# Two attention decoders on one core: the output projection's accumulator in two half-length column groups

## The chip, the cores and the metric

The kernel runs on one core of one Trainium2 chip. The core has a matrix engine (TensorE, rows PE and PEld in the profile, the second for its weight loads), a vector engine (DVE), a scalar engine (ACT), GpSimd (POOL), an engine that here only issues DMAs and waits (SP), and 16 DMA engines that carry every transfer whichever engine issued it. The metric is the device time of one execution in microseconds (us); the figure for a kernel is the median of several runs.

## The reference

Two independent decoding steps of attention, A and B, for four requests (one new token each). Their outputs lie side by side, A in columns 0 to 511 and B in columns 512 to 1023 of the result.

```
def attend(x, k_cache, v_cache, wq, wo, H, Hkv, window):      # A: H=32, Hkv=8, last 2048 keys;  B: H=32, Hkv=32, all 8192 keys
    q = (x @ wq)                                              # x: 4 x 1 x 512, wq: 512 x 4096 -> 32 heads of 128
    k, v = last `window` keys and values, repeated H/Hkv times
    p = softmax(q k^T / sqrt(128))
    o = p v                                                   # 4 x 32 x 1 x 128
    return o.reshape(4, 1, 4096) @ wo                         # wo: 4096 x 512
out = concatenate([attend(A...), attend(B...)], axis=-1)      # 4 x 1 x 1024, bf16
```

All tensors are bf16. B's keys and values are 2 x 256 MiB, and every byte of them is read once.

## The kernel before, in words

**Chunks.** The work is cut into 8 chunks of A (one key-value head with its four query heads, all four requests) and 64 chunks of B (a pair of heads `hp` of one request `b`, four chunks to a pair). Each chunk has one load of keys and one of values into the slots of `kv`. For each chunk, `keys_part` transposes the keys in groups of eight 128x128 tiles on TensorE (`emit_T`, line 406 through the helper `pe_mm`, tile `tr`), DVE or ACT copies each group to SBUF (`kt`, lines 476 and 474), and TensorE multiplies by the queries (`emit_S`, line 408, tile `sc`). `values_part` then takes the maxima, the exponentials (`exp_B`, line 575) and, interleaved, the products of the chunk before with its values (`emit_pv`, tile `po`). `norm_out` divides by the sums of the exponentials (line 664) and leaves the attention output of a head group as a small tile, `oT` for A and `oz` for B.

**The output projection.** `emit_sel` rearranges that small tile so that it fits the rows of `wo` as they were loaded (matrix products with constant selectors, then copies to `zA` or `zB`, line 681). `emit_fin` multiplies it by the loaded rows of `wo` and accumulates in the PSUM tile `fin`, a whole bank of 128 x 512 f32. B's four output rows are accumulated in partitions 0 to 3 of `fin`, A's in partitions 32 to 35, each over the full length of 512. For A there are four matmuls per chunk (weights `wor`), for B two per pair of heads-and-request chunks (weights `wos`), which `keys_part` emits in every second B chunk at group 10. Each of these matmuls has 4 stationary columns and 512 moving columns. The accumulator is opened once, in the main loop right after `emit_q(1)`, by a matmul with zeros over 36 partitions x 512 (`start` is true there and false in every `emit_fin`).

The last chunk takes a shorter way: `emit_wol` has already rearranged `wos` into `wol`, so `oz` itself is the stationary operand, and no `emit_sel` is needed.

**The output.** When the last `fin` matmul of A or of B is done, DVE copies the four rows to SBUF as bf16 (`outsb`, line 716) and one DMA of 4 x 512 elements stores them (line 718). A's is issued by ACT and B's by SP.

```
            if c == lastc:
                sch.add("dve", lambda e: e.tensor_copy(outsb[p0:p0 + NB, :], fin[p0:p0 + NB, :]), waits=[("fin", c)], key=("osb", ab))
                sch.add_dma("sp" if ab == 1 else "act",
```

**What sets the order.** A small scheduler class records, for each engine, a list of instructions with the semaphore values that they wait for; each engine works its own list strictly in order. SP's list is written first and holds all the big loads (lines 380 to 397), ending with two waits for the last `wos` and for the second half of the last keys (`kl`, line 370). Everything that is added to SP's list later comes behind these: B's output transfer, and then the two waits at the very end (lines 816 and 817) for the output semaphores `d_o0` (A) and `d_o1` (B). Some loads wait for `fin`: `dma_wo` and `dma_wos` (lines 331 and 338) overwrite weights that a `fin` matmul reads, and the loads behind them in SP's list wait as well. Key loads of B wait for the last `sc` matmul of the chunk that used the slot (line 372). The last values are loaded in five pieces (line 363), 64, 32, 16, 8 and 8 tiles, so that little work is left when the last one lands.

On TensorE, DVE and ACT the repeated chunks are emitted as loops (`emit_looped`).

## Time and profile before

| what | value |
|---|---|
| median of 5 runs | 1374.63 us |
| lowest and highest of the 5 | 1374.37 and 1375.16 us |
| profiled execution: its own time | 1374.48 us |
| profiled execution: span of the profile | 1372.7 us |
| busy: PE, PEld, DVE, ACT | 86%, 82%, 48%, 32% of the span |
| mean granted TensorE clock | 0.942 of full speed |
| HBM read | 587.21 MB, 428 GB/s over the span |
| matmuls into `fin`: A, B in the loop, B's last | 32, 64, 2, each 128x4 stationary and 512 moving columns |

The span runs from the first to the last recorded event, and 1.78 us of the execution's own time lie outside it. Busy shares are averages over the whole run, so they don't say what a stage waits for; for that the tables of waits and the chain of work that ended last are read, the chain being followed backwards from the last instruction to whatever released each step.

### The profile page before, as it was taken

To read this page: it belongs to the slowest core of one execution; us is meant where nothing else is said; L and a number is where in the kernel's file an instruction comes from. 1 tells how busy PE (TensorE), PEld (TensorE's weight loads), DVE (VectorE), ACT (ScalarE), POOL (GpSimd) and SP (SyncE) were. 2 spreads that over 40 slices of the span, in tenths; PEclk is the share of its full clock that TensorE was granted. 3 is DMA by queue.
4 is the path that set the end of the run, shared out by engine and by line. 5 is a ranking of instruction groups with operands and counts; after the bars stand their busy time and mean duration, and the time that the engine had idled before them with its cause. 6 is when DMAs were issued, how large, how long until landed. Compare 5 with 4: busy or idle time off the path is not lost.

```text
span 1372.7 us, 59835 instructions
## 1 busy us (share of the span) xinstructions
PE 1177.4 (86%) x27000; PEld 1127.1 (82%) x27001; DVE 657.0 (48%) x1434; ACT 434.7 (32%) x650; POOL 7.3 (1%) x28
## 2 busy tenths in 40 slices
PE   4888899888888988888889888888898888888988
PEld 4777898788888988888888878887888888888987
DVE  1775455444444544444445444444454444444544
ACT  1553233233223332333233323322333233223332
POOL 2000000000000000000000000000000000000000
PEclk9998999999999999999999999999999999999999
DMA  9999999999999999999999999999999999999998
GB/s 399 424 425 432 428 430 431 432 433 431 432 431 432 432 430 432 432 432 432 432 431 433 428 435 434 429 432 432 431 431 432 435 427 436 427 436 427 435 423 351
DMA packets 25253, 587.53 MB, mean 428 GB/s; under 512 B 2816, under 2 KB 2832, under 8 KB 6288
## 3 DMA queue, kind: packets, MB, share of 16 engines
q1 hardware_dynamic: 25208, 587.22, 99.7%
q8 instruction: 16, 0.26, 0.1%
q14 instruction: 5, 0.04, 0.0%
q10 hardware_dynamic: 24, 0.01, 0.0%
HBM read 587.21 MB, written 0.01 MB: 428 GB/s over the span
## 4 chain that ended last, share of the span: by engine, by line
DMA 61%; PE 36%; DVE 1%; issue 1%; ACT 1%; SPq 0%; DVEq 0%
DMA kv<-in_B_k_cache_dram 53%; PE tr L406 23%; PE sc L408 9%; DMA kv<-in_A_k_cache_dram 3%; DMA kv<-in_B_v_cache_dram 3%; PE po L408 2%; DMA kv<-in_B_wq_dram 2%; PE fin L408 2%; PE ms L408 1%; ACT kt L474 0%; DVE sA L525 0%; SPq L363 0%; ACT pba L595 0%; PE ms L406 0%; DVE zA L681 0%
## 5 line engine op out<-in xcount | busy, mean ns | idle before, releaser
L406 PE MATMUL tr<-identb,kv 128*128 128x128 bf16 x8704 | 693.5, 230 | 146.3 <-DMA kv<-in_B_k_cache_dram 140.0
L476 DVE COPY kt<-tr 128x1024 bf16<-128x1024 bf16 x736 | 502.8, 691 | 455.1 <-PE tr L406 450.7
L406 PEld LDWEIGHTS tr<-identb,kv 128*128 128x128 bf16 x8704 | 549.2, 104 | 169.2 <-DMA kv<-in_B_k_cache_dram 107.0
L474 ACT ACTIVATE kt<-tr 128x1024 bf16<-128x1024 bf16 x352 | 359.3, 1023 | 666.0 <-PE tr L406 665.8
L408 PE MATMUL sc<-qb,kt 128*128 128x64 bf16 x8704 | 444.5, 196 | 14.1 <-ACT kt L474 12.7
L408 PEld LDWEIGHTS sc<-qb,kt 128*128 128x128 bf16 x8704 | 364.3, 100 | 25.5 <-ACT kt L474 20.2
L408 PE MATMUL po<-pbb,kv 128*128 128x64 bf16 x8320 | 284.3, 192 | 6.6 <-issue 4.4
L408 PEld LDWEIGHTS po<-pbb,kv 128*128 128x128 bf16 x8320 | 263.1, 97 | 9.3 <-issue 4.6
L575 ACT ACTIVATE pbb<-sc,negb 64x128 bf16<-64x128 f32 x128 | 51.6, 403 | 254.9 <-DVE negb L562 254.2
L539 DVE TENSOR_REDUCE rm<-sc 64x1 f32<-64x128 f32 x128 | 36.9, 289 | 58.1 <-PE sc L408 57.2
L551 DVE TENSOR_REDUCE gm<-ms 1x2 f32<-1x128 f32 (+1 forms) x72 | 20.1, 279 | 48.8 <-PE ms L406 48.8
L562 DVE COPY negb<-ms 128x1 f32<-128x1 f32 (+1 forms) x72 | 11.4, 159 | 47.2 <-PE ms L408 47.2
L408 PE MATMUL ms<-identf,gx 1*128 1x1 f32 (+1 forms) x144 | 27.2, 256 | 0.8 <-DVE zA L681 0.8
L664 DVE TENSOR_TENSOR oz<-po,rz 128x8 bf16<-128x8 f32 x33 | 5.5, 167 | 43.0 <-PE po L408 43.0
L408 PEld LDWEIGHTS ms<-identf,gx 1*128 1x128 f32 (+1 forms) x144 | 21.0, 183 | 4.6 <-DVE zA L681 0.9
L575 ACT ACTIVATION_READ_ACCUMULATOR pbb<-sc,negb 64x1 f32 x128 | 23.7, 185 | 0.0
L408 PE MATMUL po<-pba,kv 128*128 128x64 bf16 x512 | 20.5, 199 | 2.8 <-ACT pba L595 1.4
L408 PEld LDWEIGHTS po<-pba,kv 128*128 128x128 bf16 x512 | 17.9, 102 | 5.6 <-ACT pba L595 4.2
L406 PE MATMUL ms<-identf,rm 128*1 128x128 f32 (+1 forms) x72 | 19.5, 271 | 2.8 <-DVE rm L534 2.8
L408 PE MATMUL fin<-wos,zB 128*4 128x512 bf16 x64 | 19.0, 378 | 0.0
L555 DVE TENSOR_SCALAR gx<-gm 1x128 f32<-1x128 f32 (+1 forms) x72 | 15.9, 221 | 2.5
L681 DVE CAST zB<-ms 64x8 bf16<-64x8 f32 x64 | 10.5, 163 | 8.9 <-PE ms L408 8.5
(61 smaller groups left out, 169.7 us busy)
## 6 DMA issues: line engine op xcount, KB each, us to landing
kv<-in_B_k_cache_dram SPq DMA_DIRECT2D x63, 4096.0 KB, 27.1
kv<-in_B_v_cache_dram SPq DMA_DIRECT2D x63, 4096.0 KB, 31.4
kv<-in_A_k_cache_dram SPq DMA_DIRECT2D x8, 2048.0 KB, 14.5
kv<-in_A_v_cache_dram SPq DMA_DIRECT2D x8, 2048.0 KB, 16.5
kv<-in_A_wq_dram SPq DMA_DIRECT2D x1, 4096.0 KB, 12.3
kv<-in_B_wq_dram SPq DMA_DIRECT2D x1, 4096.0 KB, 27.2
wor<-in_A_wo_dram SPq DMA_DIRECT2D x8, 512.0 KB, 9.9
wos<-in_B_wo_dram SPq DMA_DIRECT2D x16, 256.0 KB, 19.5
```

Source lines behind the costliest of these rows:

```text
L406: sch.add("pe", lambda e: e.transpose(o, l, r), waits, key)
L408: sch.add("pe", lambda e: e.matmul(o, l, r, start=start, stop=stop), waits, key)
L474: sch.add("act", lambda e: e.activation(dst, src, ACTF.Copy), waits=waits, key=("ev", s))
L476: sch.add("dve", lambda e: e.tensor_copy(dst, src), waits=waits, key=("ev", s))
L539: sch.add("dve", lambda e, src=src, pp=pp: e.tensor_reduce(out=rm[pp, m, 0:1], in_=src, axis=AX.X, op=ALU.max), waits=[("S", ch["s_last"]) ...
L551: sch.add("dve", lambda e: e.tensor_reduce(out=gm[0:C, m, 0:U], in_=src, axis=AX.X, op=ALU.max), waits=[("trm", c)], key=("gmax", c))
L555: sch.add("dve", lambda e: e.tensor_scalar(out=dst, in0=gv, scalar1=-scale, scalar2=None, op0=ALU.mult), waits=[("gmax", c)], key=("gx", c))
L562: sch.add("dve", lambda e: e.tensor_copy(negb[:, m, 0:C], ms[:, col:col + C]), waits=[("bc", c)], key=("negb", c))
L575: sch.add("act", lambda e, src=src, pp=pp, n=n, u=u: e.activation(probs_of(c)[pp, :, u], src, ACTF.Exp, bias=negb[pp, m, 0:1], scale=scale ...
L664: sch.add("dve", lambda e: e.tensor_tensor(out=o, in0=i0, in1=i1, op=ALU.mult), waits=waits, key=("oT", c))
L681: sch.add("dve", lambda e, src=src, pp=pp: e.tensor_copy(z[pp, :].rearrange("p (r b) -> p r b", r=k), src), waits=[("sm", c)] + free if h ...
```

## The change

`fin` is used at half its length: B's four rows are accumulated with output columns 0 to 255 in partitions 0 to 3 and columns 256 to 511 in partitions 64 to 67; A's in partitions 32 to 35 and 96 to 99. Each former matmul becomes two, with the same stationary operand and one half of the moving columns each. The opening matmul with zeros covers 128 partitions x 256. B's copy becomes one of partitions 0 to 67 x 256 (the rows between are copied along and not used); A's becomes two copies of 4 x 256. Each output becomes two DMAs of 4 x 256 elements, the first half issued by SP and the second by ACT, for A as well as for B. SP's list therefore ends with A's first half, then B's first half, then the two waits, now for two transfers on each of the semaphores. ACT's list gains B's second half at its end. The tile `outsb` has as many bytes per partition as before.

```diff
-        outsb = sb("outsb", [36, DO], BF16)
+        outsb = sb("outsb", [P, 2, DO // 2], BF16)
...
         def emit_fin(c):
             ab = 0 if 0 <= c < NCA else 1
-            p0 = 0 if ab == 1 else 32
...
             lastc = NC - 1 if ab == 1 else NCA - 1
+            at = [(0, 64), (32, 96)][1 - ab]
             for i, (l, r) in enumerate(ops):
-                pe_mm(fin[p0:p0 + NB, :], l, r, start=False, stop=i == len(ops) - 1 and c == lastc,
-                      waits=waits if i == 0 else [], key=("fin", c) if i == len(ops) - 1 else None)
+                for h, p0 in enumerate(at):
+                    pe_mm(fin[p0:p0 + NB, 0:DO // 2], l, r[:, h * DO // 2:(h + 1) * DO // 2], start=False,
+                          stop=i == len(ops) - 1 and c == lastc, waits=waits if i == h == 0 else [],
+                          key=("fin", c) if i == len(ops) - 1 and h else None)
             if c == lastc:
-                sch.add("dve", lambda e: e.tensor_copy(outsb[p0:p0 + NB, :], fin[p0:p0 + NB, :]), waits=[("fin", c)], key=("osb", ab))
-                sch.add_dma("sp" if ab == 1 else "act",
-                            lambda e: e.dma_start(out[:, 0, ab * DO:(ab + 1) * DO], outsb[p0:p0 + NB, :]),
-                            "d_o%d" % ab, waits=[("osb", ab)], key=("out", ab))
+                for rows in [slice(0, 64 + NB)] if ab == 1 else [slice(p0, p0 + NB) for p0 in at]:
+                    sch.add("dve", lambda e, rows=rows: e.tensor_copy(outsb[rows, ab, :], fin[rows, 0:DO // 2]), waits=[("fin", c)],
+                            key=("osb", ab) if rows.start == at[1] or ab == 1 else None)
+                for h, p0 in enumerate(at):
+                    x = ab * DO + h * DO // 2
+                    sch.add_dma(("sp", "act")[h], lambda e, x=x, p0=p0: e.dma_start(out[:, 0, x:x + DO // 2], outsb[p0:p0 + NB, ab, :]),
+                                "d_o%d" % h, waits=[("osb", ab)], key=("out", ab, h))
...
-                pe_mm(fin[0:36, :], pbt[0][:, 1, 0:36], pbt[0][:, 1, 0:DO], stop=False, waits=["c_sel"])
+                pe_mm(fin[:, 0:DO // 2], pbt[0][:, 1, 0:P], pbt[0][:, 1, 0:DO // 2], stop=False, waits=["c_sel"])
...
-            e.wait_ge(sems["d_o0"], 16)
-            e.wait_ge(sems["d_o1"], 16)
+            e.wait_ge(sems["d_o0"], 32)
+            e.wait_ge(sems["d_o1"], 32)
```

## The prediction

> **What bounds the kernel now.** I read the page's DMA rows first: if the transfers fill the whole span, only what runs after the last byte can change the time. The columns of the second row are packets, MB and share of 16 engines' span.

> ```profile
> DMA  9999999999999999999999999999999999999998
> ...
> q1 hardware_dynamic: 25208, 587.22, 99.7%
> q10 hardware_dynamic: 24, 0.01, 0.0%
> ```

> In all 40 slices but the last the DMA engines are at least 90% busy, and the queue that SP feeds (q1) keeps them at work 99.7% of the span. PE's 86% may hide a second bound, so next come the waits (total us, times, longest):

> ```profile
> PE tr L406 <- DMA kv<-in_B_k_cache_dram: 140.0, 57, 4.1
> SPq L718 <- DVE outsb L716: 21.6, 1, 21.6
> SPq L817 <- DMA out_dram<-outsb: 0.9, 1, 0.9
> ```

> TensorE waits for B's keys 57 times, 140.0 / 57 = 2.46 us each: it has room in nearly every chunk. The other two rows belong to the end: SP had come to the output transfer 21.6 us before it could issue it, and waited 0.9 us for it to land. So the third view is the chain of work that ended last, from its last transfer on, in order of time (start, us, what):

> ```profile
> 1330.22 38.66 DMA kv<-in_B_v_cache_dram
> 1368.88 0.05 issue
> 1368.92 0.42 PE po L408 x8
> ...
> 1369.44 0.18 DVE oz L664
> ...
> 1369.66 0.61 PE fin L408 x2
> 1370.27 0.02 issue
> 1370.29 0.68 DVE outsb L716
> ```

> The last piece of values lands at 1368.88. From there everything is in series: eight products, the division, two `fin` matmuls, the copy, and from 1371.00 (the timeline's start of SP's output DMA) 1.70 us of transfer and closing to 1372.70. That tail is 3.82 us, and the change touches its last three links. The table by stretch (busy us and instructions of PE, PEld, DVE, ACT, POOL, then clock, DMA share, GB/s) shows that nothing competes with it:

> ```profile
> 1330.00:1368.90 38.90, 36.15 (x894) 34.26 (x892) 19.04 (x41) 12.65 (x19) 0.00 (x0) 1.00 0.94 398
> 1368.90:1372.70 3.80, 1.00 (x10) 0.38 (x10) 0.85 (x2) 0.00 (x0) 0.00 (x0) 1.00 0.00 1
> ```

> TensorE has its full clock (1.00) there, and the DMA engines are empty (share 0.00).

> **The change, part by part.** First the tail, where every hundredth counts. The prices are in the groups by shape (busy, mean ns | idle before):

> ```profile
> L408 PE MATMUL fin<-wos,zB 128*4 128x512 bf16 x64 | 19.0, 378 | 0.0
> L716 DVE CAST outsb<-fin 4x512 bf16<-4x512 f32 x2 | 1.4, 680 | 2.6 <-PE fin L408 2.6
> L695 DVE CAST wol<-tr 128x512 bf16<-128x512 f32 x1 | 0.7, 693 | 0.5 <-PE tr L408 0.5
> L438 DVE CAST qs<-ms 128x128 bf16<-128x128 f32 x2 | 0.6, 292 | 14.8 <-PE ms L408 14.8
> ```

> *Copy.* The same kind of copy costs 292 ns for 128 columns and 693 for 512, so 401 / 384 = 1.044 ns a column. Partitions hardly count: 4 of them take 680 ns where 128 take 693. 256 columns cost 292 + 128 x 1.044 = 426 by the tall rows and 680 - 256 x 1.044 = 413 by the flat one; for 68 partitions I take 0.42. Saved: 0.68 - 0.42 = **0.26 us**. Bounds: 0.39 (as short as the 128-column row) and 0.

> *Matmuls.* Two of 512 columns become four of 256. The timeline gives the two together 0.59 us and one 0.378, so the second starts 0.21 after the first: that is what 512 columns occupy, and 256 occupy 0.107. A last one of 256 takes about 0.27 by the line through the 64-column products (0.192) and the 512-column row (0.378). If the four go one after the other, 3 x 0.107 + 0.27 = 0.59: nothing is saved. If the two halves of a pair, which use different columns of the array and different partitions of PSUM, run beside each other, 0.107 + 0.27 = 0.38, and **0.21 us** is saved. The upper end is the weight loads: before, the two of 82 ns each are done within 0.09 (the timeline), beside the matmuls; two more that nothing hid would add 2 x 0.08 = 0.16. No row shows matmuls in two column groups, so the ends are -0.21 and +0.16. I take -0.21: pairs that share neither columns nor partitions have no reason in this trace to queue, and the row of overlapped weight loads is the nearest. [...]

> *Transfers.* One DMA of four rows of 1 KB becomes two of 512 B rows, on SP and on ACT. The timeline shows 0.35 us of issue on SP; the DMA table of 1371.76 to 1371.95 holds all eight packets (four rows, four signals), and 1371.00 to 1371.76 holds none. So 0.95 us passes from issue to last packet, of which only 0.19 is transfer, spread over rows that start one after the other. Halving the rows can't save more than about 0.1; two transfers of four rows queueing behind each other would add those 0.19 again; and A's issue on ACT took 0.28, less than SP's. ACT is free: its last work is the 0.60 us `wol` activation at 1364.49. Ends -0.1 and +0.3 (0.19 and a tenth for one more wait); I take **0**, since the two issues run beside each other.

> [...]

> Now everything ahead of the last byte. In the loop each pair of B chunks gets four half matmuls for two whole ones: -0.21 to +0.16 us of PE, against about 2.5 us of waiting for keys in each chunk. If that cover were gone, 32 x 0.21 = 6.7 us would show. `fin` also releases the loads of `wos` and `wor`, with SP's later loads queued behind them; but a 4 MB key load lands 27.1 us after issue and at the 431 GB/s of a typical slice takes 9.7, so some 17 us of transfers stand ahead of it, and a few tenths don't empty the queue. A's last copy becomes two of about 0.41, +0.15 us of DVE at 124 us; DVE then sat idle 0.28 before the next key copy. The opening matmul runs beside the copy of the queries, which ends later (33.13 against 32.73 + 0.21 of columns). A's first half is now issued by SP behind all loads, about 1349.4 (21.6 us before 1371.00), where SP only waited: its 0.35 us are hidden, its four rows stand behind the last values in the queue, and its landing is long over when SP waits for it. Its second half stays where A's transfer was, on ACT at 124 us. All of this: 0.

> **Sum.** 1374.48 (the profiled execution: span 1372.70 and 1.78 around it) - 0.26 - 0.21 + 0 = 1374.01. The median of the five runs lies 0.15 above the profiled execution, so for a median I expect 1374.63 - 0.47 = **1374.16 us**, 0.03% less. A measurement of this kernel tells a difference from none at about 0.2%, 2.7 us; this one is far below.

> **Rivals.**

> 1. *The pairs don't overlap*, so the halves don't do what the partitions are for. For it: no row shows such an overlap, and matmuls start in order. Against: disjoint columns. Then only the copy counts: 1374.63 - 0.26 = 1374.37, or 1374.5 with unhidden weight loads.
> 2. *ACT's transfer comes late*, on the other side. The one output transfer ACT issued before, A's at 124.23, had no packet before 127.7, and its eight packets ran until 129.65 (DMA tables of these stretches): 5.4 us from issue, against SP's 0.95. If that belonged to ACT's queue, the end would come 5.4 - 0.95 - 0.47 = 4.0 us later: 1378.6. It decides as soon as ACT's transfer takes more than 0.95 + 0.47 = 1.42 us. Against it: at 124 us the DMA engines were 101% busy with loads, and at the end they are empty; at the start of the span ACT's first DMA, issued at 0.81 on empty engines, had packets by 2.2.
> 3. *TensorE's path through `fin` sets the pace after all*, since the chain does pass `fin` (0.53 us each) on its way to key loads. Then 32 x 0.21 would come off as well: 1374.16 - 6.7 = 1367.5. Against it: 99.7%, and 424 to 436 GB/s in every slice but the first and the last.

> **Chances.** Forecast 0.57; no overlap 0.32; ACT late 0.06 (half of it by enough for over 0.2%); pace of TensorE 0.02; anything else 0.03, mostly within 0.2%. So faster by over 0.2% has 0.02, within 0.2% 0.95, slower 0.03. The range takes the unknown ends, copy 0.39, matmuls 0.21, transfers 0.1 below (1374.63 - 0.70 = 1373.9), +0.16 and +0.3 with the copy's 0.26 above (1374.83), and the spread of the runs around their median (0.26 below, 0.53 above): 1373.6 to 1375.3.

> **What would show it.** In the profile after: the tail's `outsb` copy at 0.41 to 0.43; the four `fin` matmuls at about 0.38 from the first start to the copy, against 0.6 without overlap, with starts in pairs; ACT's output issue beside SP's; SP's last wait still about 0.9 us, and the span's end about 3.35 us after the last values land instead of 3.82. The DMA share stays 99.7%. Wrong would be: an end wait well over 1 us, or a last landing that moves by more than a few tenths, which would mean that the loop and not the tail had changed.

## The result: 0.2% slower, with a shorter tail

The changed kernel takes 1377.86 us (median of 23 runs, 1376.35 to 1379.06), the kernel before in the same measurement 1375.01 us (43 runs, 1374.27 to 1375.58). The ratio is 1.002, with a 95% interval of 1.0015 to 1.0026. 1374.2 had been forecast and at most 1375.3.

The profiled execution of the changed kernel took 1376.26 us, 1.78 more than that of before, with a span of 1374.5 us against 1372.7. It is the shortest execution of all, so it shows less of the loss than the median. The chain of work that ended last, from the last load of values on:

```profile
1332.12 38.91 DMA kv<-in_B_v_cache_dram
1371.03 0.05 issue
1371.08 0.42 PE po L408 x8
...
1371.59 0.18 DVE oz L664
...
1371.81 0.40 PE fin L408 x4
1372.21 0.02 issue
1372.24 0.42 DVE outsb L721
```

The tail did what was forecast: `fin` 0.40 us where it was 0.61, the copy 0.42 where it was 0.68. From the last landing to the end of the span 1374.5 - 1371.03 = 3.47 us pass, where it was 3.82. But the last values land at 1371.03 and not at 1368.88. So 2.15 us were lost ahead of the tail and 0.35 won in it: 1.80, the difference of the spans.

Where they were lost is found by asking which wait of TensorE is new. Before, between 118 and 200 us (total, times, longest):

```profile
PE po L408 <- issue: 4.4, 2, 2.7
PE fin L408 <- DVE zA L681: 0.8, 1, 0.8
PE tr L406 <- issue: 0.6, 1, 0.6
```

After, the same view:

```profile
PE tr L406 <- issue: 7.1, 2, 5.8
PE po L408 <- issue: 3.0, 1, 3.0
PE fin L408 <- DVE zA L681: 0.8, 1, 0.8
```

"issue" is time in which the engine waited for nothing that the profile shows, no data and no other engine. One such wait of 5.8 us is new. TensorE's timeline puts it exactly between A's last `fin` matmuls and B's first transposes. Before, these follow each other without a wait:

```profile
121.61 1.87 PE L408 MATMUL fin<-wor,zA 128*4 128x512 bf16 x4 [0.81 <-DVE zA L681]
123.41 2.32 PE L406 MATMUL tr<-identb,kv 128*128 128x128 bf16 x24
```

After:

```profile
121.39 0.60 PE L408 MATMUL fin<-wor,zA 128*4 128x256 bf16 x8 [0.81 <-DVE zA L681]
127.81 2.74 PE L406 MATMUL tr<-identb,kv 128*128 128x128 bf16 x24 [5.83 <-issue]
```

In the DMA table of the changed kernel from 122 to 127.8 us one transfer is of another kind than the loads (packets, MB, share):

```profile
q1 hardware_dynamic: 84, 2.49, 100.2%
q8 instruction: 1, 0.02, 1.2%
```

A 16 KB piece of instructions was on its way (its packet ran from 124.9 to 126.0 us), and it had to share the DMA engines with loads that filled them: q1 alone took 100.2% of the 16 engines' time. (That queue q8 carries TensorE's list is shown by run e7 below: only TensorE's list is laid out differently there, and q8 has 152 packets where it had 16.) The piece alone proves nothing: before, one passes at the same time, here in the table of 124.5 to 128 us:

```profile
q8 instruction: 1, 0.02, 1.9%
```

But there B's transposes had begun at 123.41, before it came, so their own piece was there already. The difference is the number. From 118 to 200 us there are 7 such pieces before and 8 after, and over the whole run also one more. Before:

```profile
q8 instruction: 16, 0.26, 0.1%
```

After:

```profile
q8 instruction: 17, 0.28, 0.1%
```

How a stall on TensorE turns into lost transfer time, in a kernel whose DMA engines are always busy, is seen in SP's timeline. The next key load waits for a `sc` matmul. Before:

```profile
120.21 0.33 SPq L372 DMA_DIRECT2D kv<-in_B_v_cache_dram  x1
134.82 0.33 SPq L372 DMA_DIRECT2D kv<-in_B_k_cache_dram  x1
```

After:

```profile
120.00 0.33 SPq L372 DMA_DIRECT2D kv<-in_B_v_cache_dram  x1
139.73 0.33 SPq L372 DMA_DIRECT2D kv<-in_B_k_cache_dram  x1
```

The issue comes 4.9 us later, and the loads behind it follow late. The queue then runs dry in part: at its worst from 160 to 165 us, where the DMA engines are busy 0.72 of the time at 252 GB/s, against 0.98 and 416 before. The stretch from 140 to 165 us (clock, DMA share and GB/s are the last three numbers), first before:

```profile
140.00:165.00 25.00, 20.00 (x419) 18.99 (x416) 9.57 (x21) 6.66 (x13) 0.00 (x0) 0.86 1.01 428
```

and after:

```profile
140.00:165.00 25.00, 20.43 (x486) 19.73 (x487) 10.76 (x25) 6.11 (x10) 0.00 (x0) 0.93 0.93 378
```

50 GB/s less over 25 us are 1.25 MB, 2.9 us at the full rate. From 165 to 200 us a little comes back (432 GB/s against 429): counted from 118 to 200 us, 33.99 MB have passed where it was 35.12, 1.13 MB or 2.6 us less. 2.15 us of that remain at the last landing; the rest is too little to be seen in the rates (431 GB/s in both kernels from 200 to 1330 us).

### The profile page after: what moved, and what is told of

It reads as the page before. It is cut to its first block, busy times and chain, and to the rows that moved or that the text cites. A ratio compares the mean times of both kernels' runs of the same rounds, so it can differ in the third digit from the quotient of the medians.

```text
span 1374.5 us, 60034 instructions
## 1 busy us (share of the span) xinstructions
PE 1174.1 (85%) x27098; PEld 1135.3 (83%) x27099; DVE 657.3 (48%) x1435; ACT 435.2 (32%) x650; POOL 7.3 (1%) x28
## 2 busy tenths in 40 slices
DMA  9999999999999999999999999999999999999998
## 3 DMA queue, kind: packets, MB, share of 16 engines
q1 hardware_dynamic: 25216, 587.22, 99.7%
## 4 chain that ended last, share of the span: by engine, by line
DMA 61%; PE 35%; ACT 1%; issue 1%; DVE 1%; SPq 0%; DVEq 0%
DMA kv<-in_B_k_cache_dram 56%; PE tr L406 22%; PE sc L408 9%; DMA kv<-in_B_v_cache_dram 3%; PE po L408 2%; DMA kv<-in_B_wq_dram 2%; PE fin L408 1%; ACT kt L474 1%; ACT pba L595 1%; PE ms L408 1%; DVE sA L525 1%; DVE rm L534 0%; DVE sA L523 0%; PE ms L406 0%; SPq L363 0%
## 5 line engine op out<-in xcount | busy, mean ns | idle before, releaser
L406 PE MATMUL tr<-identb,kv 128*128 128x128 bf16 x8704 | 699.7, 231 | 149.4 <-DMA kv<-in_B_k_cache_dram 139.2
L406 PEld LDWEIGHTS tr<-identb,kv 128*128 128x128 bf16 x8704 | 554.4, 104 | 164.6 <-DMA kv<-in_B_k_cache_dram 92.6
L408 PE MATMUL sc<-qb,kt 128*128 128x64 bf16 x8704 | 447.1, 196 | 13.7 <-ACT kt L474 12.8
L408 PEld LDWEIGHTS sc<-qb,kt 128*128 128x128 bf16 x8704 | 367.7, 100 | 23.7 <-ACT kt L474 20.2
L408 PE MATMUL po<-pbb,kv 128*128 128x64 bf16 x8320 | 284.0, 192 | 5.5 <-issue 3.0
L408 PEld LDWEIGHTS po<-pbb,kv 128*128 128x128 bf16 x8320 | 263.0, 97 | 8.0 <-issue 3.1
L408 PE MATMUL ms<-identf,gx 1*128 1x1 f32 (+1 forms) x144 | 27.4, 257 | 0.8 <-DVE zA L681 0.8
L664 DVE TENSOR_TENSOR oz<-po,rz 128x8 bf16<-128x8 f32 x33 | 5.5, 167 | 43.4 <-PE po L408 43.4
L408 PEld LDWEIGHTS ms<-identf,gx 1*128 1x128 f32 (+1 forms) x144 | 21.3, 184 | 4.7 <-DVE zA L681 0.9
L408 PE MATMUL po<-pba,kv 128*128 128x64 bf16 x512 | 20.5, 199 | 4.9 <-ACT pba L595 3.1
L408 PEld LDWEIGHTS po<-pba,kv 128*128 128x128 bf16 x512 | 17.9, 102 | 7.1 <-ACT pba L595 5.0
L406 PE MATMUL ms<-identf,rm 128*1 128x128 f32 (+1 forms) x72 | 19.6, 273 | 3.6 <-DVE rm L534 3.5
L408 PE MATMUL ms<-xT,kv 128*128 128x4 bf16 x256 | 7.1, 166 | 8.9 <-DMA kv<-in_B_wq_dram 4.4
## 6 DMA issues: line engine op xcount, KB each, us to landing
kv<-in_A_wq_dram SPq DMA_DIRECT2D x1, 4096.0 KB, 12.3
```

The source lines that it names most:

```text
L406: sch.add("pe", lambda e: e.transpose(o, l, r), waits, key)
L408: sch.add("pe", lambda e: e.matmul(o, l, r, start=start, stop=stop), waits, key)
```

## The experiments

Theory A (code): the change makes TensorE's instruction list 32 instructions longer ahead of B's loop. Each matmul is a weight load and a multiplication (27,001 and 27,000 records before); A has four more matmuls per chunk, with two chunks in its loop and two in the straight code behind it. That pushes the end of the straight code over the border of a 16 KB piece, and B's loop, which is put at the start of a piece, moves on by one. What a piece holds can be counted in the trace of before: 256, 512 and 256 records of TensorE lie between the waits for `issue` that end at 135.98, 143.00, 157.68 and 163.73 us, and 16 packets of q8 carry 0.26 MB, so a piece is 256 instructions and 16 KB. Theory B (work): the second column group, A's two copies or A's two transfers hold TensorE up. Intervals are those of the ratio to the kernel before, measured beside it.

**e1: the halves without the column groups.** The kernel before with every `fin` matmul in two halves, in the old partitions:

```diff
-                pe_mm(fin[p0:p0 + NB, :], l, r, ...)
+                for h in range(2):
+                    x = slice(h * DO // 2, (h + 1) * DO // 2)
+                    pe_mm(fin[p0:p0 + NB, x], l, r[:, x], ...)
...
```

> The kernel before, with only one part of the change: each matmul into fin is made in two halves of 256 columns, both in the partitions that it used before. No second column group, one copy of 512, one output transfer each. Theory A (code): the change is slower because TensorE's instruction list is 32 instructions longer ahead of B's loop, so that one more 16 KB instruction transfer is needed there and TensorE stands still about 5.8 us at 122 us. This kernel has the same number of TensorE instructions as the changed one, so the stall must be there, 17 instruction packets instead of 16, and the time is 2 to 4 us above the kernel before, 1376.5 to 1379. Theory B (work): the stall comes from the second column group, from A's two copies or from A's two transfers at that place. Then none here: 1374.3 to 1375.6, 16 packets. In the tail both theories expect that halves in one column group run one after the other: four matmuls from first start to the copy in 0.60 to 0.64 us, where the changed kernel needs 0.40 to 0.42.

1377.81 us, ratio 1.0022 (1.0013 to 1.0032), 17 instruction packets, and the stall (TensorE's timeline):

```profile
121.68 1.03 PE L408 MATMUL fin<-wor,zA 128*4 128x256 bf16 x8 [0.81 <-DVE zA L681]
129.15 2.10 PE L406 MATMUL tr<-identb,kv 128*128 128x128 bf16 x18 [6.44 <-issue]
```

So neither the column groups nor the copies nor the transfers are needed for the loss. The tail tells the other thing: in one column group four halves take 0.60 us, as two whole ones did,

```profile
1373.84 0.60 PE L408 MATMUL fin<-wol,oz 128*4 128x256 bf16 x4 [0.33 <-DVE oz L664]
```

where the changed kernel's four take 0.38 and the copy follows 0.43 us after their start, here 0.63. The 0.2 us come from the column groups, not from the halving.

**e2: only B changed.** `at` is `(0, 64)` for B and `(32,)` for A, with A's matmuls, copy and transfer at full length, and an opening matmul of 128 x 512.

> The changed kernel with A as it was before: A's matmuls, copy and transfer at full length, only B in two halves, two column groups and two transfers. TensorE's list ahead of B's loop then has as many instructions as before the change. Theory A (code): no stall at 122 us, 16 instruction packets, and the gain of the tail is left: 0.3 to 0.4 us below the kernel before, 1374.0 to 1375.2. Theory B, with the column groups of B in the loop as the cause: 1376.5 to 1379, since B's part is unchanged; with A's copies or transfers as the cause: as theory A.

1374.14 us against 1374.83 of the kernel before, ratio 0.9996 (0.9987 to 1.0005), 16 instruction packets, and no stall:

```profile
121.36 1.02 PE L408 MATMUL fin<-wor,zA 128*4 128x512 bf16 x4 [0.81 <-DVE zA L681]
123.30 1.51 PE L406 MATMUL tr<-identb,kv 128*128 128x128 bf16 x24 [0.92 <-DMA kv<-in_B_k_cache_dram]
```

B's column groups in the loop cost nothing. The interval takes in no change, so a gain over the kernel before is not proved by the times; its shortest run (1373.89 against 1374.33) is 0.44 us shorter, near the 0.35 of the changed kernel's tail. Against the changed kernel's 1377.86 it is plainly faster.

**e3: all of the change, another place for the loop.** The last number is the slot, in a piece of 256 instructions, at which B's loop begins. At 48 the straight code can run on into the loop within one piece.

```diff
-            sch.emit_looped("pe", e, sems, loop_on(mybir.EngineType.PE, (None, 0)))
+            sch.emit_looped("pe", e, sems, loop_on(mybir.EngineType.PE, (None, 48)))
```

> The changed kernel with all of its work; only the place of TensorE's second loop in its instruction list differs: its first instruction is put at slot 48 of an instruction block, where the changed kernel puts it at slot 0. The straight code ahead of the loop, which by theory A ends in the first 32 slots of a block, then runs into the loop within the same block instead of jumping over the rest of it. Theory A (code): the stall of 5.8 us at 122 us goes, 16 instruction packets, time 0.3 to 0.4 us below the kernel before: 1374.0 to 1375.2. Theory B (work): nothing changes, 1376.5 to 1379.

16 packets, and at the border TensorE waits only for keys:

```profile
121.64 1.02 PE L408 MATMUL fin<-wor,zA 128*4 128x256 bf16 x8 [0.81 <-DVE zA L681]
123.45 2.74 PE L406 MATMUL tr<-identb,kv 128*128 128x128 bf16 x24 [0.79 <-DMA kv<-in_B_k_cache_dram]
```

That is theory A, and theory B falls with it: the same work, and the stall is gone. But the time, 1375.74 us, ratio 1.0006 (0.9997 to 1.0015), lies above the expected 1375.2, with runs from 1374.13 to 1377.85. Two other stalls grew inside B's first two chunks, in the profile of the longest of these runs:

```profile
144.44 0.37 PE L408 MATMUL ms<-identf,gx 1*128 1x1 f32 x1 [3.94 <-issue]
168.22 1.14 PE L408 MATMUL po<-pbb,kv 128*128 128x64 bf16 x18 [4.71 <-issue]
```

Run e9 asks what they are.

**e4, e5, e6: the kernel before with instructions added far away.** 16, 4 or 8 tiny matmuls with zeros ahead of the opening one, at 33 us, so 32, 8 or 16 instructions:

```diff
+                for i in range(16):
+                    pe_mm(fin[0:4, i:i + 1], pbt[0][:, 1, 0:4], pbt[0][:, 1, 0:1], waits=["c_sel"] if i == 0 else [])
...
```

> The kernel before, with 16 extra matmuls of one column and four rows with zeros, right ahead of the opening matmul of fin at 33 us (which clears what they wrote). They add as many instructions to TensorE's list as the change does ahead of B's loop, 90 us before the place of the stall and in no other way alike. Theory A (code): the stall appears all the same between A and B, at about 122 to 128 us, with 17 instruction packets, and the time is 2 to 4 us above the kernel before, 1376.5 to 1379. Theory B (work): at most the 16 matmuls' own 1 us at 33 us, hidden by the transfers: 1374.3 to 1375.6.

> As e4_pad16, with 4 extra matmuls in place of 16, so 8 instructions more ahead of B's loop instead of 32. Theory A (code) as a threshold: only crossing the border of a 16 KB instruction piece costs anything. e4 crossed it with 32. With 8 it is crossed only if fewer than 8 instructions of room were left; in a room of at most 32 I give that one chance in four. Either it isn't crossed: 16 instruction packets, no stall near 122 us, 1374.3 to 1375.6; or it is, with the full stall of 5 to 6.5 us and 17 packets, 1376.5 to 1379. Rival theory A2 (each instruction more costs its share of the time): a quarter of e4's loss, 1375.4 to 1375.8, and a stall of 1.5 us.

> As e4_pad16, with 8 extra matmuls, 16 instructions more ahead of B's loop. Theory A as a threshold: all or nothing, as in e5, with equal chances: either no stall at 122 us, 16 packets and 1374.3 to 1375.6, or the full stall of 5 to 6.5 us, 17 packets and 1376.5 to 1379. Rival theory A2 (a share for each instruction): half of e4's loss, 1376.1 to 1376.4, and a stall of about 3 us.

With 16: 1377.73 us, ratio 1.0019 (1.0010 to 1.0028), 17 packets, and the stall at the same place, though nothing there was touched:

```profile
121.62 1.02 PE L408 MATMUL fin<-wor,zA 128*4 128x512 bf16 x4 [0.81 <-DVE zA L681]
128.06 2.74 PE L406 MATMUL tr<-identb,kv 128*128 128x128 bf16 x24 [5.42 <-issue]
```

With 4: 1374.56 us (ratio 0.9989 to 1.0008); with 8: 1374.67 (0.9991 to 1.0010). Both have 16 packets and no stall at the border. Theory A2, a share of the loss for each instruction, had expected a stall of 1.5 us with 4 and of about 3 us with 8, and with 8 at least 1376.1, where the interval ends at 1376.0: it falls. (With 4 it had expected 1375.4 to 1375.8, which the interval of the time alone, up to 1375.7, doesn't exclude.) It is a threshold, somewhere above 16 and at most 32 instructions away.

**e7: the kernel before with B's loop at slot 224.** `(None, 0)` becomes `(None, 224)`, and nothing else.

> The kernel before with not one instruction of work more; only the first instruction of TensorE's second loop is put at slot 224 of a 256-instruction block instead of slot 0. Theory A, in its closer form: a piece of 256 instructions is fetched when TensorE enters the piece ahead of it, the fetch takes about 5 to 6 us beside the loads, and a piece with few instructions in it gives TensorE too little to do meanwhile. The loop then starts with a piece of 32 instructions, so TensorE must stand still 4 to 6 us some 16 matmuls after the start of B, near 123 us; 17 instruction packets; 1376 to 1379. If instead the cost hung on the jump over the rest of a block, or on more instructions, there would be no stall within B's first 30 matmuls and 1374.3 to 1376.

The stall came, 14 matmuls into B:

```profile
123.81 1.67 PE L406 MATMUL tr<-identb,kv 128*128 128x128 bf16 x14
128.72 1.23 PE L406 MATMUL tr<-identb,kv 128*128 128x128 bf16 x10 [3.24 <-issue]
```

So a piece with few instructions in it is enough; no jump at that spot is needed. That a packet comes after TensorE has entered the piece ahead of it can be read from the trace of before: q8's seven packets start at 125.2, 133.5, 140.7, 146.8, 155.2, 161.2 and 168.6 us, the first 1.8 us after the loop's start at 123.41, the third, fourth, sixth and seventh 3.5 to 4.9 us after the waits' ends at 135.98, 143.00, 157.68 and 163.73. The stall's 3.2 us are less than the 4 to 6 expected, and the time missed by far: 1538.57 us, ratio 1.1181 (1.1158 to 1.1204). The page of this run says why:

```profile
q1 hardware_dynamic: 25208, 587.22, 91.3%
q8 instruction: 152, 2.49, 0.6%
```

One pass of the loop is about 1607 instructions, by the records of TensorE in the trace of before from one loop branch to the next (780 weight loads, 780 multiplications, the rest registers, semaphores and the branch). From slot 0 they lie in seven pieces of 256 (the unit in which the slot is counted); from slot 224 they end near 224 + 1607 = 1831 and lie in eight. With seven no piece is fetched between 200 and 1330 us; with eight, pieces are fetched again and again, 136 packets more in all, and the keys' transposes alone wait 170.9 us for `issue`, once in each of the 32 passes:

```profile
PE tr L406 <- issue: 170.9, 32, 7.8
```

**e8: both output halves on SP.** e2 with `eng = "sp"` for both halves of B.

> e2_only_b with both halves of B's output issued by SP, one after the other, instead of one by SP and one by ACT. If two transfers cost only their issue, the second leaves one issue, 0.27 to 0.35 us, later, so the end comes 0.25 to 0.35 us later from SP's first issue than in e2, where it is 1.84 us (1371.06 to 1372.90): 2.1 to 2.2 us, and 1374.4 to 1374.5 in all. If the issues hide behind the first transfer's latency of 0.7 us, the end comes at most 0.1 us later, and ACT's share in the change is worth nothing.

SP's two issues took 0.67 us:

```profile
1371.56 0.67 SPq L726 DMA_DIRECT2D out_dram<-outsb  x2
```

From 1371.56 to the end of the span (1373.60) it is 2.04 us, against 1.84 in e2. So the second issuing engine is worth 0.2 us in these two profiles, a little less than one issue. That lies between the two cases of the expectation, 0.25 to 0.35 us and at most 0.1. The time, 1374.79 us (ratio 0.9990 to 1.0009), can't tell so little.

**e9: the kernel before at slot 48.** As e3, on the kernel before.

> The kernel before with TensorE's second loop put at slot 48 instead of slot 0, as in e3 but with nothing of the change. It tells what e3's remaining loss is (1375.74 against the 1374.2 that was expected, with stalls of 3.9 and 4.7 us inside B's first pair of chunks). If it belongs to the place of the borders between the pieces of 256 instructions in the loop (now 48 instructions later in the work, in the stretches where TensorE runs through its list fastest), this kernel shows stalls of 3 to 5 us at the same two places, 16 packets, and 1375.0 to 1376.5. If it belongs to the change's work, there are only the stalls of up to 2.7 us of the kernel before, and 1374.3 to 1375.0.

1375.97 us, ratio 1.0009 (0.9999 to 1.0019), runs from 1374.45 to 1378.49, where the kernel before beside it had 1374.34 to 1375.55; 16 packets, and the larger waits sit at e3's two places:

```profile
142.07 0.27 PE L408 MATMUL ms<-identf,gx 1*128 1x1 f32 x1 [2.84 <-issue]
165.13 1.04 PE L408 MATMUL po<-pbb,kv 128*128 128x64 bf16 x16 [4.10 <-issue]
```

One is a little under the 3 to 5 us expected, and the intervals of e3 and e9 both touch 1, so the size of the loss is not settled. Its kind is, for what remained in e3 needs nothing of the change. That the waits sit at borders between pieces can be counted for the first. Before, the wait of 2.7 us there comes two `ms` and 23 `po` matmuls after the same point:

```profile
139.12 0.38 PE L408 MATMUL ms<-identf,gx 1*128 1x1 f32 x2
139.43 0.85 PE L408 MATMUL po<-pbb,kv 128*128 128x64 bf16 x23
143.00 1.09 PE L408 MATMUL po<-pbb,kv 128*128 128x64 bf16 x17 [2.72 <-issue]
```

In e9 it comes after one `ms`, so 24 matmuls earlier. With their weight loads these are 48 instructions, just the shift.

## Why the prediction was wrong, point by point

- *The copy*, 0.26 us saved: 0.42 us was forecast and 0.42 measured. Right.
- *The matmuls*, 0.21 saved by the overlap of two column groups: right (0.61 to 0.40 in the chain). No row of before showed the overlap; it was the author's estimate, and e1 shows it as the reason: four halves took 0.38 us in two groups, 0.60 in one.
- *The transfers*, taken as 0, with ends of -0.1 and +0.3: 1371.00 to 1372.7 was 1.7 us before, 1372.68 to 1374.5 is 1.8 after; SP's last wait is 1.1 us, where it was 0.9. So about +0.1, within the ends, and the tail as a whole won 0.35 instead of 0.47.
- *Everything ahead of the last byte: "All of this: 0."* This step failed: the last values landed 2.15 us later. That is the sign that the prediction itself had named as wrong, a last landing that moves by more than a few tenths. Of the parts that it named none is needed for the loss (e4), and all of them together do without the stall at the border (e3). What it left out is that the added matmuls are also code. It priced their execution and not their place in the list, although the page showed 16 instruction transfers on the same DMA engines, and the waits showed TensorE standing still for `issue`, 2.7 us at the longest between 118 and 200 us, without a reason in data. In its place the runs showed one more piece of the list to be fetched at that border, and TensorE standing still there for 5.8 us.
- *The cover of "some 17 us of transfers"* was sound for a few tenths, but it was applied to the steady loop alone. At the border between A and B the queue is shorter: a key load that landed 27.1 us after its issue in the loop (the median) landed in 17.1 there, before the change, in the DMA table of 130 to 180 us. A stall of 5.8 us went through in part. The share over the whole span did not show it: q1 stands at 99.7% in both kernels, while 25 us of the changed one ran at 0.93. So the first sentence of the prediction, by which full transfers leave only what comes after the last byte, took an average for every stage.
- *The rivals.* Missing overlap and a late ACT transfer were wrong: ACT's issue at 1372.69 was followed by all 16 packets of both transfers between 1373.4 and 1373.6, so 0.9 us, far from the 1.42 at which that rival decided. The pace of TensorE through `fin` did not set the time either: the loop has 0.2 us less of it per pair of chunks (12.3 us of `fin` in 32 pairs, before 19.0), and the loads' queue kept the DMA engines busy 99.7% of the span as before. The side that had 3 chances in 100 came true, though only just (0.21% by the medians), and through a mechanism that none of the rivals held.

## What to carry to other kernels

The added matmuls could cost twice here: by their execution, which stayed hidden in the loop (e2, ratio 0.9996), and by their place in TensorE's list, which shifts all the code behind it: 32 instructions more brought a wait of 5.4 us (e4, ratio 1.0019), 16 more none (e6). Where a kernel fills the DMA engines, as this one does for 99.7% of its span, count the instruction packets, look for waits put down to `issue` at the change from one loop to the next, and find how far the list is from the next 16 KB border before calling a few more matmuls free. If a change is slower for no reason in its own work, pad the list of the old kernel: e4 separated code from work in one run. Moving the loop does so less cleanly, since in e3 and e9 it brought longer waits at other borders.
